# A feed-forward block begun with its first 256 rows, attention maxima turned on 64x32 tiles, and splits moved to VectorE, in a fused adaLN, attention and GLU kernel

## The chip, the cores and the metric

The kernel runs on one core of one Trainium2 chip. The time is that of the device, in microseconds from the start to the end of one execution. Before the change it is 1716.86 us, the median of three runs (1716.64 to 1719.71).

## The reference

One sequence of 2048 rows with 512 values each goes through attention and then through a gated feed-forward block, each behind a norm that is scaled and shifted by values computed from a condition vector `c`.

```python
mod = (silu(c) @ w_mod).reshape(1, 6, 1, 512)
sa, ca, ga, sb, cb, gb = ...
h = layernorm(x) * (1 + ca) + sa
q = heads(h @ wq)              # 32 heads of 16
k, v = h @ wk, h @ wv          # one head of 16, shared
p = softmax(q @ k.T * 16 ** -0.5)
x = x + ga * ((p @ v) @ wo)
h = layernorm(x) * (1 + cb) + sb
x = x + gb * ((sigmoid(h @ w_gate) * (h @ w_up)) @ w_down)   # 1792 wide
```

All is float32. The kernel splits most operands of its products into a high and a low float16 part and adds three products (high by high, high by low, low by high).

## The kernel before, in words

**A prologue** (`PLAN`) computes the norm, `k`, `v` and the first six of sixteen query groups, and writes the queries to DRAM (`qD`).

**The loop.** The queries are cut into 8 blocks of 256 rows (`NQ`), each with 4 groups of 8 heads (`NU`): 32 *units* (`units`, index `i`; block `b`, group `o`). A unit has 16 *steps*, one for each block of 128 keys (`NKB`), so there are 512 steps, `s`. A step has two halves (`h`), and `ORDER` fixes what each half issues:

- two tiles `sa` (scores with the queries on the partitions), 21 steps ahead of their use; VectorE reduces each 128x512 tile to its maxima (`mx`, in `a_max`);
- two tiles `st` (scores with the keys on the partitions, with the maximum subtracted through two extra rows of `qp`); ScalarE turns each into `P` with `Exp` (`st_tile`);
- one product `craw` of `P` with `V` in float32, two steps later (`pv`);
- one *piece* of other work (`piece`).

TensorE is used as eight tiles of 64 rows by 32 columns: `columns` (L133 is the line through which every operation of the prologue and loop is recorded) issues one product as four matmuls, one for each 32 columns of the output. `sa` and `st` of a half use one half of the rows, `craw` the other.

**Maxima.** Once a unit's last score tile is issued, `max_end` reduces `mx` (128 partitions, 8 heads x 2 blocks of 128 queries x 4 key chunks) to `m16` of 128x16, and `max_rows` turns it with one float32 matmul against the identity into 16x128, scales it on ScalarE, splits it into `mh`, and four DMAs on SP's queue write it into rows of `qp`.

**Other work: Groups, Couples, terms.** A `Group` is an accumulation of terms into one PSUM bank; a `Couple` runs two Groups together, each *term* on both halves of the rows, that is eight matmuls of 64x32 by 512 columns. The feed-forward work of a *pair* of query blocks (512 rows, `ffn_groups`) is: two Couples `wo` of 24 terms (the projection), the norm of the four row tiles (`norm`, `norm2`, `normed`, through `defer`, which runs a function some steps later), four pieces `tr` of transposes (`Transposes`, `tr_part`) whose result `split_evac` evicts as `h2` high and low, fourteen Couples `gu` of 24 terms (gate and up for one 128-wide chunk of 1792, one bank each), four of them behind two Couples `dn` of 48 terms, and at the end two of 36: 552 terms. In the norm, the sum `xr` and all after the statistics run on GpSimd (POOL), `bn_stats` on VectorE. Gate and up weights come from DRAM (`wD`) by `load_gw`, 512 KB a chunk, into `GWB` buffers.

**The planner.** `plan` picks a Couple when no piece is left, and `places` spreads its terms over the coming halves: `RATE` 2.2 terms a half, at most about 3; query Couples before step `FIRST` go at `QRATE` and skip three halves. `pick` takes the head of the list `main`: `wo` from nine steps (`SKIP`) after it was listed, `tr` two steps (`GAP`) after the norm's mark, others when the list `spare` is empty. Otherwise it takes from `spare`, where the five query Couples lie at first and where the last two `dn` Couples of each pair go (`KEPT`), to fill the time in which the next pair waits. A pair is listed when its second query block has been finished, at steps 128, 256 and 384. A Couple that wouldn't end within the loop isn't begun.

**Weights.** `weight_jobs` loads and splits `wo`, gate, up and down on POOL, 42 jobs over `WSTEPS` = 110 steps, and the last four (they overwrite the query weights) three steps apart from step `WLAST`.

**The tail** works without tiles (L184: 128x128 by 512 columns): the rest of `wo` of the fourth pair, `last_unit`, the first Couple left over, the end of `wo` (with norm), all others left over, the transposes, and the fourth pair's gate, up and down.

Of the kernel before, what the change touches and what calls it, by code (L numbers as in the profile page):

```python
# [16 lines left out]
P = 128  # L17
# [5 lines left out]
QB = 512  # L23
# [52 lines left out]
W1 = 2  # L76
W2 = 3
# [1 line left out]

PBUFS = 4  # L80
SBANKS = {"st": 2, "sa": 3}
GWB = 3
HBUFS = 36


# [1 line left out]
def adaln_mqa_glu_kernel(  # L87
# [39 lines left out]
    class Ordered:  # L127
        def __init__(self, engine):
            self.engine = engine
# [220 lines left out]
    def split_evac(src, k, sc, sh, hi, lo):  # L350
        h32 = t32("h32")[:, :QU]
        act.activation(h32, src, AF.Identity, scale=sc[:, k:k + 1], bias=sh[:, k:k + 1])
        pool.tensor_scalar(hi, h32, 1.0, 0.0, op0=ALU.mult, op1=ALU.add)  # L353
        pool.tensor_tensor(lo, h32, hi, op=ALU.subtract)  # L354


# [243 lines left out]
    pend = []  # L600

    def max_end(i):
        m16 = wp.tile([P, 16], F32, tag="m16", name="m16", bufs=4)
        dve.tensor_reduce(m16.rearrange("p (h t) -> p h t", t=2), mxs[i], axis=AX.X, op=ALU.max)
        return lambda: max_rows(i, m16)

    def max_rows(i, m16):
        qp = get_q(i)
        pm = sbank("sa")
        pe.matmul(pm[:16, :P], m16, ident, start=True, stop=True)  # L610
        m32 = wp.tile([16, P], F32, tag="m32", name="m32", bufs=4)
        act.activation(m32, pm[:16, :P], AF.Identity, scale=1.0 / SM)
        mh = wp.tile([16, 2, P], F16, tag="mh", name="mh", bufs=4)
# [127 lines left out]
    def defer(n, f_):  # L741
        waits.append((now[0] + n, f_))
# [34 lines left out]
    class Transposes:  # L777
        stage, n = "tr", 4

        def __init__(self, part):  # L780
            self.part = part

        def alone(self):
            self.part(0, 4)
# [1 line left out]
    def ffn_groups(b):  # L786
# [4 lines left out]
        gws = {}  # L791
        ths = {}
        fs = [*range(4, NFC), *range(4)]

        def wo_group(t):
            def term(n, rs):
# [24 lines left out]

        def norm(t, t1, xr):
            pool.tensor_tensor(xr, t1, xr, op=ALU.add)
# [12 lines left out]

        pts2 = {}

# [14 lines left out]
        def load_gw(f):  # L853
            if f < NFC:
                gws[fs[f]] = gw_tile()
                sp1.dma_start(gws[fs[f]], wD[fs[f]])

        def gu_group(p, m):
            def term(n, rs):
                k, i = divmod(n, 3)  # L860
                gw = gws[fs[p]]
                w_, h_ = passes(gw[:, 2 * m], gw[:, 2 * m + 1], *h2[k])[i]
                return w_[rs, k, :], h_[rs]

            def end(p_, second):
                if m == 0:
                    ths[p] = th = t32("th")
                    act.activation(th, p_, AF.Tanh, scale=0.5 / (SH * SW))  # L868
                else:
                    th = ths.pop(p)  # L870
                    if second:
                        u_ = t32("u")
                        dve.tensor_copy(u_, p_)
                        pool.tensor_scalar(th, th, 1.0, 1.0, op0=ALU.add, op1=ALU.mult)  # L874
                        pool.tensor_tensor(th, th, u_, op=ALU.mult)
                    else:
                        dve.scalar_tensor_tensor(th, th, 1.0, p_, op0=ALU.add, op1=ALU.mult)
                    hi, lo = t16("gh"), t16("gl")
                    pool.tensor_scalar(hi, th, 1.0, 0.0, op0=ALU.mult, op1=ALU.add)
                    pool.tensor_tensor(lo, th, hi, op=ALU.subtract)  # L880
                    gT[fs[p]] = (hi, lo)

            return Group("gu", 12, "pgu", term, end, (lambda: load_gw(p + GWB - 1)) if m == 0 else None)

        HF = 8

        def down_group(t, lo):
            n_ = HF if lo == 0 else NFC - HF
# [23 lines left out]
            return Group("dn", 3 * n_, "pd", term, end)  # L912

        wos = [wo_group(t) for t in range(4)]
        trs = [Transposes(lambda n0, n1, u=u, z=z: tr_part(u, z, n0, n1)) for u in range(2) for z in range(2)]
        gs = []
        for lo, hi in ((0, HF), (HF, NFC)):
            gs += [Couple(gu_group(p, 0), gu_group(p, 1)) for p in range(lo, hi)]
            gs += [Couple(down_group(t, lo), down_group(t + 1, lo)) for t in (0, 2)]
        return wos, trs, gs  # L920


    alist = [(i, n) for i in range(len(units)) for n in range(64)]
# [81 lines left out]
    first_rows = []  # L1005

    def pick(s):
        if first_rows and s >= (len(units) - NU) * NKB + SKIP:
            return first_rows.pop()
        while main and main[0][0] is None:  # L1010
            main.pop(0)
            spare.extend(z[1] for z in main[:KEPT])
            del main[:KEPT]
        if main:
            b, g = main[0]
            if g.stage == "tr":
                ok = b in marks and s >= marks[b] + GAP
            elif g.stage == "wo":
                ok = s >= g.ready + SKIP
            else:  # L1020
                ok = not spare
            if ok:
                return main.pop(0)[1]
        return spare.pop(0) if spare else None


    def plan(s, hb):
# [6 lines left out]
        if g.stage == "tr":  # L1034
            sizes = [4]
        else:
            q = g.stage == "q" and s < FIRST
            rate, most = (QRATE, 1) if q else (RATE, MOST)
            sizes = []
            for leg in range(2):  # L1040
                sizes += places(g.n // 2, hb + len(sizes), rate, most, (3 if leg == 0 else 0) if q else None, g.w)
            if hb + len(sizes) > 2 * len(units) * NKB:
                spare.insert(0, g)
                return
# [17 lines left out]
    for i, (b, o) in enumerate(units):  # L1062
        if o == 0 and b == NQ - 1:
            ends = ffn_groups(NB - 1)
            first_rows.append(Couple(*ends[0][:2]))
        if o == 0 and b > 0 and b % 2 == 0:
            pair = b // 2 - 1
            wos, trs, gs = ffn_groups(pair)
            gs = [Couple(*wos[:2]), Couple(*wos[2:])] + trs + gs
            for g in gs[:2]:  # L1070
                g.ready = i * NKB
            main.extend([(pair, g) for g in gs[:-KEPT]] + [(None, None)] + [(pair, g) for g in gs[-KEPT:]])
        for kb in range(NKB):
            s = i * NKB + kb
            now[0] = s
# [51 lines left out]
    del psum["s"]  # L1127
    pinned.clear()
    tail.append(True)
    wos, trs, gs = ends  # L1130
    assert not first_rows
    wos = wos[2:]
    for g in wos:
# [41 lines left out]
```

## Time and profile before

| what | us |
|---|---|
| median of three runs | 1716.86 |
| the profiled execution | 1717.44 |
| its span, first to last instruction | 1715.4 |
| start of the first `P` (step 0) | 109.0 |
| end of the last `P` (step 511) | 1553.3 |

The profiled execution is 2.0 us longer than its span, and 0.6 us longer than the median. The loop's 2048 tiles `P` mark its steps: four to a step. A view of windows counts them, and the time of a window over a quarter of its tiles is the time of one step. Matmuls overlap, so a busy TensorE says little: what a term costs is seen in the length of the steps and in the chain of work that ended last.

### The profile page before, as it was taken

Reading aid. Unit: us, or ns where it says so; the run is one execution under the profiler, and the core shown is the slowest. Engines: PE = TensorE matmul, PEld = TensorE weight load, DVE = VectorE, ACT = ScalarE, POOL = GpSimd, SP = SyncE. Lnnn points to the kernel's source line nnn. Section 1 sums busy time; section 2 is a strip of 40 time slices with the busy share of each in tenths; the row PEclk is TensorE's granted clock in tenths of the full one; section 3 lists DMA queues with packets and bytes.
Section 4 is the critical chain, followed back from the end, with each engine's and each line's share of the span. In section 5 each row is a group of like instructions: output and inputs, shape, how many; then the busy total and the mean of one; then the engine's idle time right before and its main releaser. Section 6 shows DMA issues by size and latency. Waiting matters only on the chain.

```text
span 1715.4 us, 88057 instructions
## 1 busy us (share of the span) xinstructions
PE 1667.8 (97%) x39888; PEld 996.6 (58%) x39888; DVE 1409.5 (82%) x2364; ACT 1290.5 (75%) x2335; POOL 616.3 (36%) x812
## 2 busy tenths in 40 slices
PE   6999999999999999999999999999999999999998
PEld 3335554555564667666765666666666666654443
DVE  7799999999998999999998999999998999802111
ACT  5448988999987888888887888888888888882100
POOL 4432545452047332132254222233364233221523
PEclk9989999999999999999999999999999999999999
DMA  7111323321022111010121110010112110011211
GB/s 247 47 61 48 102 94 111 92 70 33 15 64 63 49 45 32 12 50 27 28 65 52 52 40 28 25 44 20 38 50 63 47 57 15 24 50 47 82 54 49
DMA packets 84675, 94.06 MB, mean 55 GB/s; under 512 B 22868, under 2 KB 63820, under 8 KB 84300
## 3 DMA queue, kind: packets, MB, share of 16 engines
q1 hardware_dynamic: 84300, 88.44, 16.6%
q8 instruction: 312, 5.11, 1.2%
q14 instruction: 63, 0.52, 0.1%
HBM read 67.82 MB, written 16.24 MB: 49 GB/s over the span
## 4 chain that ended last, share of the span: by engine, by line
PE 85%; DVE 5%; ACT 3%; POOL 3%; DMA 1%; issue 1%; SPq 1%; POOLq 0%; ACTq 0%; DVEq 0%
PE craw L133 23%; PE pgu L133 15%; PE sa L133 14%; PE st L133 13%; PE pd L133 6%; PE pgu L184 5%; DVE mx L133 3%; PE pd L184 3%; PE po L133 2%; PE pq L133 2%; ACT P L133 2%; SPq L133 1%; DMA lc<-lD 1%; POOL h2l L354 1%; DMA xall<-in_A_x_dram 1%
## 5 line engine op out<-in xcount | busy, mean ns | idle before, releaser
L133 DVE TENSOR_REDUCE mx<-sa 128x1 f32<-128x512 f32 x2048 | 1293.4, 683 | 99.2 <-PE st L133 43.5
L133 ACT ACTIVATE P<-st 128x512 f32<-128x512 f32 x2048 | 1166.7, 598 | 221.3 <-PE st L133 163.9
L133 PE MATMUL craw<-P,V 64*32 64x512 f32 x8192 | 1096.2, 601 | 1.2 <-PE craw L133 0.2
L133 PE MATMUL sa<-kp,qp 64*32 64x512 f16 (+1 forms) x7940 | 837.0, 379 | 10.9 <-DVE mx L133 10.3
L133 PE MATMUL st<-qp,kp 64*32 64x512 f16 x8192 | 838.6, 380 | 7.9 <-ACT P L133 6.2
L133 PEld LDWEIGHTS <-kp 64*32 64x32 f16 x8192 | 336.4, 91 | 227.9 <-issue 105.7
L133 PEld LDWEIGHTS <-qp 64*32 64x32 f16 (+1 forms) x7940 | 286.0, 92 | 132.6 <-issue 55.1
L133 PE MATMUL pgu<-h2h,gw 64*32 64x512 f16 x4992 | 268.8, 377 | 3.4 <-POOL h2h L353 2.6
L133 PEld LDWEIGHTS <-gw 64*32 64x32 f16 x7488 | 171.6, 92 | 69.1 <-issue 29.4
L133 PEld LDWEIGHTS craw<-P,V 64*32 64x32 f32 x8192 | 184.7, 105 | 26.9 <-ACT cs L133 4.6
L133 PE MATMUL craw<-nought 64*32 64x1 f16 x1048 | 171.2, 163 | 0.0
L133 PE MATMUL pgu<-h2l,gw 64*32 64x512 f16 x2496 | 167.4, 377 | 1.0 <-POOL h2l L354 1.0
L133 PEld LDWEIGHTS <-nought 64*32 64x32 f16 x1048 | 97.8, 93 | 72.0 <-issue 53.4
L874 POOL TENSOR_SCALAR th<-th 128x512 f32<-128x512 f32 x39 | 24.2, 620 | 315.3 <-ACT th L133 263.3
L554 POOL MEMSET qp<- 32x1024 f16 x60 | 56.6, 944 | 117.8 <-PE st L133 83.7
L184 PE MATMUL pgu<-h2h,gw 128*128 128x512 f16 x272 | 81.4, 379 | 2.2 <-POOL h2h L353 2.2
L318 POOL TENSOR_SCALAR wst<-wst 128x512 f32<-128x512 f32 x46 | 28.4, 618 | 153.5 <-DMA wst<-in_B_w_up_dram 106.4
L868 ACT ACTIVATE th<-pgu 128x512 f32<-128x512 f32 x17 | 10.1, 597 | 94.3 <-PE pgu L184 94.1
L133 PE MATMUL pd<-wdl,gh 64*32 64x512 f16 x1152 | 75.7, 376 | 0.0
L133 PE MATMUL pd<-wdh,gh 64*32 64x512 f16 x1152 | 75.0, 376 | 0.2
L133 PE MATMUL pd<-wdh,gl 64*32 64x512 f16 x1152 | 73.7, 376 | 0.0
L704 POOL TENSOR_TENSOR raw<-raw 128x256 f32<-128x256 f32 x31 | 22.7, 732 | 139.1 <-DMA raw<-lD 131.6
(159 smaller groups left out, 1438.7 us busy)
## 6 DMA issues: line engine op xcount, KB each, us to landing
gw<-wD SPq DMA_DIRECT2D x56, 512.0 KB
wD<-gw SPq DMA_DIRECT2D x14, 512.0 KB
wm<-in_w_mod_dram SPq DMA_DIRECT2D x6, 1024.0 KB
qp<-qD SPq DMA_DIRECT2D x192, 32.0 KB
qD<-q SPq DMA_DIRECT2D x16, 256.0 KB
xr<-in_A_x_dram SPq DMA_DIRECT2D x16, 256.0 KB
out_dram<-ot SPq DMA_DIRECT2D x16, 256.0 KB
raw<-cs SPq DMA_DIRECT2D x248, 16.0 KB
```

Of the source, the lines that this page charges most:

```text
L133: return (lambda *a, **k: keep(f_(*a, **k))) if pinned else f_
L184: pe.matmul(cut[0](self.bank) if cut else self.bank, l_, r_, start=(n == 0), stop=(n == self.n - 1))
L318: pool.tensor_scalar(w_, w_, SW, 0.0, op0=ALU.mult, op1=ALU.add)
L354: pool.tensor_tensor(lo, h32, hi, op=ALU.subtract)
L554: eng.memset(qp[j:j + 32], 0.0)
L704: keep(pool.tensor_tensor(raw[:, :QU], raw[:, :QU], raw[:, QU:], op=ALU.mult))
L868: act.activation(th, p_, AF.Tanh, scale=0.5 / (SH * SW))
L874: pool.tensor_scalar(th, th, 1.0, 1.0, op0=ALU.add, op1=ALU.mult)
```

## The change

- Each of the first three pairs is listed in two parts. When the first of its query blocks is finished (steps 64, 192, 320), its first `wo` Couple, the two transposes of these 256 rows and Couples `gu_half` are listed: gate and up of two chunks at once, each product 256 columns wide, 48 terms at a weight of one half. `AHEAD` = 4, 3, 3, 0 Couples of this kind, that is 8, 6, 6 and 0 chunks. When the second block is finished (128, 256, 384), the other `wo`, its transposes, the same chunks for the other 256 rows (the weights are loaded again), the rest of gate and up, and `dn` follow.
- Before step 137 such a Couple goes at `ERATE` = 1.2 (at most 2) instead of 2.2.
- Query Couples go at 0.9 a half instead of 0.45, and count as early before step 77 instead of 136; the last four weight jobs begin at step 115 instead of 150.
- `norm2` comes two steps after `norm` instead of one. A mark is set for each 256 rows, and the transposes alternate between them.
- `split_evac` makes the high part with a copy on VectorE instead of on POOL.
- `max_end` makes two reductions of 64 partitions, and the turn is a matmul of 64 rows by 32 columns over 64 columns; `mh` is 32x64, and each DMA takes 16 rows of it.
- `GWB` is 4 instead of 3, and weights are asked for one Couple further ahead.

```diff
-QRATE = 0.45
+QRATE = 0.9
+ERATE = 1.2
+AHEAD = 4, 3, 3, 0
-WLAST = 150
+WLAST = 115
-FIRST = 136
+FIRST = 77
-GWB = 3
+GWB = 4
...
     def split_evac(src, k, sc, sh, hi, lo):
         h32 = t32("h32")[:, :QU]
         act.activation(h32, src, AF.Identity, scale=sc[:, k:k + 1], bias=sh[:, k:k + 1])
-        pool.tensor_scalar(hi, h32, 1.0, 0.0, op0=ALU.mult, op1=ALU.add)
+        dve.tensor_copy(hi, h32)
         pool.tensor_tensor(lo, h32, hi, op=ALU.subtract)
...
-        m16 = wp.tile([P, 16], F32, tag="m16", name="m16", bufs=4)
-        dve.tensor_reduce(m16.rearrange("p (h t) -> p h t", t=2), mxs[i], axis=AX.X, op=ALU.max)
+        m16 = wp.tile([64, 32], F32, tag="m16", name="m16", bufs=4)
+        for u in range(2):
+            dve.tensor_reduce(m16.rearrange("p (h t u) -> p h t u", t=2, u=2)[:, :, :, u], mxs[i][64 * u:64 * u + 64],
+                              axis=AX.X, op=ALU.max)
...
-        pe.matmul(pm[:16, :P], m16, ident, start=True, stop=True)
+        pe.matmul(pm[:32, :64], m16, ident[:64, :64], start=True, stop=True)
...
-                    sp1.dma_start(qp[r:r + 1], mh[8 * j:8 * j + 8, h, :])
+                    sp1.dma_start(qp[r:r + 1], mh[16 * j:16 * j + 16, h, :])
...
+        ahead = 2 * AHEAD[b]
+        uses = [(p, 0) for p in range(ahead)]
+        uses += [(p, None) for p in range(NFC)]
...
-            defer(1, lambda: norm2(t, t1, xr))
+            defer(2, lambda: norm2(t, t1, xr))
...
-            if t == 3:
-                marks[b] = now[0]
-                for f in range(GWB - 1):
-                    load_gw(f)
+            if t % 2 == 1:
+                marks[b, t // 2] = now[0]
+            if t == (1 if ahead else 3):
+                ask(2 if ahead else GWB - 1)
...
+        def gu_half(p, m, u, at):
+            us = slice(u * QU, (u + 1) * QU)
+
+            def term(n, rs):
+                e, (k, i) = n // 12, divmod(n % 12, 3)
+                gw = gws[at + e]
+                w_, h_ = passes(gw[:, 2 * m], gw[:, 2 * m + 1], *h2[k])[i]
+                return w_[rs, k, :], h_[rs, us], lambda z: z[:, e * QU:(e + 1) * QU]
+
+            def end(p_, second):
+                gated(p, m, p_, second, [(e, us, slice(e * QU, (e + 1) * QU)) for e in range(2)])
+
+            return Group("gu", 24, "pgu", term, end, (lambda: ask(at + GWB)) if m == 0 else None, w=0.5)
...
+        es = [Couple(gu_half(p, 0, 0, p), gu_half(p, 1, 0, p)) for p in range(0, ahead, 2)]
+        gs += [Couple(gu_half(p, 0, 1, at + p), gu_half(p, 1, 1, at + p)) for p in range(0, ahead, 2)]
...
-            rate, most = (QRATE, 1) if q else (RATE, MOST)
+            light = not q and g.stage == "gu" and s < 2 * NU * NKB + SKIP
+            rate, most = (QRATE, 1) if q else (ERATE, 2) if light else (RATE, MOST)
...
-        if o == 0 and b > 0 and b % 2 == 0:
-            pair = b // 2 - 1
-            wos, trs, gs = ffn_groups(pair)
-            gs = [Couple(*wos[:2]), Couple(*wos[2:])] + trs + gs
...
+        if o == 0 and b % 2 == 1 and b < NQ - 1:
+            blocks[b // 2] = ffn_groups(b // 2)
+            wos, trs, _, es = blocks[b // 2]
+            main.extend([*ready(b // 2, [Couple(*wos[:2]), trs[0], trs[2]], i), (None, len(es)), *ready(b // 2, es, i)])
+        if o == 0 and b % 2 == 0 and b > 0:
+            wos, trs, gs, _ = blocks.pop(b // 2 - 1)
+            gs = [Couple(*wos[2:]), trs[1], trs[3], *gs]
+            main.extend([*ready(b // 2 - 1, gs[:-KEPT], i), (None, KEPT), *ready(b // 2 - 1, gs[-KEPT:], i)])
```

More of the change, by code (lines that the diff above doesn't have):

```diff
@@ L778, in adaln_mqa_glu_kernel, with __init__ @@
         stage, n = "tr", 4
-        def __init__(self, part):
-            self.part = part
+        def __init__(self, part, u):
+            self.part, self.u = part, u
         def alone(self):
@@ L865, in end @@
             def end(p_, second):
[L866 to L885, printed above, removed]
+                gated(p, m, p_, second, [(0, slice(0, QB), slice(0, QB))])
+            return Group("gu", 12, "pgu", term, end, (lambda: ask(at + GWB)) if m == 0 else None)
         def down_group(t, lo):
@@ L1003, in places, with ready @@
         return [k - z for z, k in zip([0] + ends, ends)]
-    first_rows = []
+    first_rows, blocks = [], {}
+    def ready(pair, gs, i):
+        for g in gs:
+            g.ready = i * NKB
+        return [(pair, g) for g in gs]
     def pick(s):
@@ L1010, in pick @@
         while main and main[0][0] is None:
-            main.pop(0)
-            spare.extend(z[1] for z in main[:KEPT])
-            del main[:KEPT]
+            n = main.pop(0)[1]
+            spare.extend(z[1] for z in main[:n])
+            del main[:n]
         if main:
@@ L1129, in adaln_mqa_glu_kernel @@
     tail.append(True)
-    wos, trs, gs = ends
+    wos, trs, gs, _ = ends
     assert not first_rows
```

57 lines of the change are left out of this document (40 added, 17 removed).

## The prediction

> **What bounds the kernel now.** I read the windows first, cut at the units of the loop by the times of the tiles `P`: for `P` alone, then for all engines (columns: window, its us, busy us and count of PE, PEld, DVE, ACT and, in the second, POOL, granted clock, DMA share, GB/s). In the first view VectorE has no column, since it touches no `P`.
>
> ```profile
> 109.00:478.80 369.80, 304.46 (x2280) 45.02 (x2280) 320.58 (x576) 0.99 0.22 67
> 624.60:809.50 184.90, 136.71 (x1028) 24.52 (x1024) 147.56 (x257) 1.00 0.12 35
> ```
> ```profile
> 109.00:478.80 369.80, 364.23 (x8143) 191.25 (x8140) 357.68 (x603) 330.69 (x610) 138.37 (x176) 0.99 0.22 67
> 624.60:809.50 184.90, 184.48 (x5474) 125.70 (x5467) 171.86 (x279) 154.61 (x279) 51.85 (x59) 1.00 0.12 35
> 1553.30:1715.40 162.10, 152.71 (x727) 69.55 (x722) 29.52 (x50) 14.91 (x27) 54.29 (x64) 1.00 0.18 59
> ```
>
> 576 tiles are 144 steps: 369.8 / 144 = 2.57 us a step while only queries run beside the attention, and VectorE is busy for 97% of it. 256 tiles (the 257th is the next window's) are 64 steps: 2.89 us a step while gate, up and down run; VectorE is at 93%, ScalarE at 84%. There the matmuls number 5474; 16 each of `sa`, `st` and `craw` a step make 3 x 1028, and some 130 are hand-overs, so (5474 - 3084 - 130) / 8 = 282 terms ran, 4.4 a step. The early window has 120 query terms over some 140 steps, 0.83 a step, with matmuls counted the same way. So **a term costs (2.89 - 2.57) / (4.4 - 0.83) = 0.09 us in the loop**: early VectorE sets the pace and TensorE has room, later they share it.
>
> The tail is another matter. The chain of work that ended last shows it:
>
> ```profile
> 1563.83 6.91 PE pgu L184 x32
> 1570.73 1.30 PE po L184 x6
> 1572.03 8.63 PE pgu L184 x40
> 1580.66 15.55 PE pd L184 x72
> 1597.01 1.26 POOL ot L905
> 1599.39 1.11 POOL h2h L353 x3
> 1602.56 40.31 PE pgu L184 x186
> ```
>
> 72 matmuls take 15.55 us, **0.216 us a term**. The 32 + 40 `pgu` and 72 `pd` ahead of 1602.56 are 144 terms of the third pair that the loop had no room for. A term moved from the tail into the loop is worth 0.216 - 0.09.
>
> Third, three places in the loop are slower than their neighbours, each at the norm and the transposes of a pair (again `P` alone):
>
> ```profile
> 517.20:546.50 29.30, 19.39 (x136) 2.76 (x128) 17.98 (x32) 0.88 0.21 66
> 908.60:922.60 14.00, 7.32 (x52) 1.32 (x48) 6.75 (x12) 0.88 0.34 102
> 1280.30:1292.90 12.60, 6.58 (x56) 1.05 (x48) 7.18 (x13) 1.00 0.22 56
> ```
>
> 8, 3 and 3 steps at 2.89 us would be 23.1, 8.7 and 8.7: **15.4 us of stalls**. In the chain of the second one the work passes to POOL:
>
> ```profile
> 908.85 1.28 POOL ot L899
> 910.13 2.46 POOL ot L905 x2
> 912.59 0.38 POOL h2h L353
> 913.05 0.67 POOL h2l L354
> ```
>
> POOL finishes the eviction of `dn` first, then makes eight high and eight low parts, and gate and up wait.
>
> **The change part by part**, against the profiled execution's 1717.4 us (0.6 above the median).
>
> *Terms in the first 137 steps.* Five query Couples at 0.9 instead of 0.45 end by step 76. Then come one `wo` Couple (24 terms), two transposes, and four half Couples of 48 x 0.5 at 1.2 a half, ten steps each, so all four end near step 131. That is 240 terms there instead of 112, and 128 x 0.09 = 11.6 us. From below: TensorE has room, and the step pays only what VectorE gets.
>
> ```profile
> L133 DVE TENSOR_TENSOR t<-po,ga 128x512 f32<-128x512 f32 x7 | 4.8, 681 | 0.0
> L133 DVE BATCH_NORM_STATS2 st<-xr 128x6 f32<-128x512 f32 x14 | 9.6, 684 | 3.7 <-POOL xr L823 3.5
> L133 DVE BATCH_NORM_AGGREGATE mv<-st 128x2 f32<-128x6 f32 x30 | 5.5, 182 | 1.0
> L133 DVE COPY u<-pgu 128x512 f32<-128x512 f32 x39 | 26.6, 682 | 38.6 <-PE pgu L133 38.6
> ```
>
> One 0.68, two 0.68 + 0.18 and four 0.68 are 5.1 us, and four copies for the splits 1.4 more (below): 6.5. **I take +9.** The faster queries give VectorE nothing; ScalarE and POOL evict them.
>
> *Terms after step 137.* By the planner's rules 1524 instead of 1544 run there: 20 x 0.09, **-1.8**. In the list above, work of the next pair is now listed when a pair ends some 27 steps sooner, so the loop stays filled; two waits of eight steps for a norm remain empty (near 142 and 272).
>
> *The tail.* Of 1680 terms (3 x 552 and the fourth pair's first `wo`) the planner's rules leave one `dn` Couple, 36 terms, at the loop's end. So 108 x 0.216 = 23.3 us go. But the 24.2 us of work from 1572.03 to 1596.21 covered the norm of the last two row tiles, whose VectorE part the timeline bounds:
>
> ```profile
> 1571.49 0.69 DVE L811 TENSOR_TENSOR t<-po,ga 128x512 f32<-128x512 f32 x1 [1.70 <-PE po L184]
> 1578.87 0.55 DVE L348 TENSOR_SCALAR t<-xr,mv,rs 128x512 f32<-128x512 f32 x1
> ```
>
> 1579.4 - 1572.0 = 7.4 us are bare once no work is left there; what is late next is the transposes. Half of these (256 rows ready long before) fit in the wait, and of the 6.35 us from 1596.21 to 1602.56 some 2.3 go with that half and with POOL's high parts. The first Couple left over grows from 24 to 36 terms: 2.6. So -24.2 + 7.4 - 2.3 + 2.6 = **-16** (from -23.3, nothing bare, to -9, if the wait is twice as long).
>
> *Stalls.* The eight high parts leave POOL (0.40 us of 1.07 each), the rows come in halves, the last weight jobs leave the first stall, and the order lets `dn` run behind the transposes of the first halves of pairs two and three. Against it, there are six places instead of three. I take 1 us at each: **-10** (from -15.4 to +15.4, should all six stay as long).
>
> *The split on VectorE* isn't in the trace with this shape. The nearest rows:
>
> ```profile
> L133 DVE CAST wkvh<-wkv 128x128 f16<-128x128 f32 x1 | 0.2, 226 | 0.0
> L353 POOL TENSOR_SCALAR h2h<-h 128x256 f16<-128x256 f32 x32 | 12.6, 404 | 0.7 <-ACT h L133 0.7
> ```
>
> It lies between 0.23 (half as wide, the same operation) and 0.68 (twice as wide, out of PSUM, above); I take 0.35, by the first. Twenty in the windows where VectorE is at 93% find room. The copy is an added wait: VectorE stands until ScalarE has made `h`, behind one `Exp` at most, and the next maxima queue up behind it, for which `sa` waits once three banks are full. The -10 above holds this.
>
> *Maxima.* Per unit:
>
> ```profile
> L133 DVE TENSOR_REDUCE m<-mx 128x16 f32<-128x64 f32 x32 | 7.0, 219 | 1.0
> L133 DVE TENSOR_TENSOR mh<-m,mh 16x128 f16<-16x128 f32 x32 | 11.0, 345 | 3.4 <-ACT mh L133 3.4
> L133 PE MATMUL sa<-ident,m 128*16 128x128 f32 x64 | 12.5, 278 | 0.0
> ```
>
> A second reduction adds up to 0.22 on VectorE, 64 columns for 128 in `mh` take up to 0.17 off, and the matmul no longer needs both halves of the rows (up to 0.56 of 2 x 0.278). Over 32 units that is from -23 to +7. Near VectorE's rows, **+2** for these and the late copies. The Trainium skill, TensorEngine Tiling, Key Properties, says that a change of tiling mode drains TensorE; by it the turn would save more than its own time, towards the lower end. No row here isolates a drain.
>
> *Products of 256 columns.* 960 terms of half width stand where 480 ran, 768 of them after step 137, each with its own eight weight loads. Two take as long as one of 512 if the loads (0.092 us) hide under 0.108 of stream:
>
> ```profile
> L133 PEld LDWEIGHTS <-gw 64*32 64x32 f16 x7488 | 171.6, 92 | 69.1 <-issue 29.4
> 1548.48 0.40 PE L133 MATMUL st<-qp,kp 64*32 64x512 f16 x4
> 61.67 1.30 PE pv L133 x48
> ```
>
> Four tiles whose matmuls take 0.38 each are through in 0.40, so tiles start some 7 ns apart; a full array with short products starts one every 1.30 / 48 = 27 ns. If the latter held for tiles too, a half term would take 8 x 27 ns = 0.216, no less than a whole one. From 0 to 768 x 0.108 = +83 us; the second row has the kernel's own tiles, so I stay near it: **+4** (5 ns each).
>
> The 20 chunks loaded twice are 10 MB more where DMA is at 0.12 to 0.22; each is asked for one Couple ahead. A load that waits for its buffer holds up on SP's queue the rows of `mh`, `place` and the loads of `raw` behind it; these have two steps or more. I cost them at nothing, and at up to a step a Couple, 20 x 2.9, if the cover goes.
>
> **Sum:** +9 - 1.8 - 16 - 10 + 2 + 4 = -12.8; 1717.4 - 12.8 = 1704.6, and 0.6 less for the median: **1704**.
>
> **The rivals.**
>
> *Slower: tiles have an issue floor.* In the 90 steps with half terms after 137, 8.5 of them a step with 50 other matmuls make 118; at 27 ns that is 3.2 us against 2.89, and +0.31 x 90 = 28. It decides from 24.4 ns a matmul (2.89 / 118) on. 1704 - 4 + 28 = **1728**; with all of the +83, 1783. For it: that row, and that the kernel never needed more: 184.9 us / 5474 is 34 ns a matmul. Against it: the row of four tiles in 0.40. Chance 0.2. The Trainium skill, TensorE: Matmul & The Clock Gate, "Wait — 56ns, not 53.3ns?", gives a floor of about 25 ns from start to start however narrow the product; the trace agrees on the full array. By that figure a half term is 0.2, 118 matmuls 2.95 us, and the time 1704 - 4 + 0.06 x 90, an estimate of 1705. The same page's span model has some 4 ns for each further tile, and by that nothing is added.
>
> *Slower: six stalls for three.* A wait takes the place of the one removed: if the transposes' evictions hold each of six places for 5.1 us, +15.4 replaces -10: **1729**. For it: the chain ends at `h2l`, which stays on POOL. Against: half the rows at a time. Chance 0.1.
>
> *No gain: the leftovers were cover.* If the norm's wait is twice as long (tail -9), the early terms cost 11.6 and the stalls give 8 back: 1704 + 7 + 2.6 + 2 = **1715.6**. For it: the bare norm is one chain over VectorE and POOL, with nothing beside it; against it, its 7.4 us were measured with other work on VectorE. Chance 0.13.
>
> *More.* Early terms at 6.5, the tail at -20, stalls at -15, turns at -3: **1687**. For it: the early window is VectorE's (97%), so its own sum may be all that counts there. Chance 0.17.
>
> **How the numbers follow.** The forecast (1696 to 1712) has 0.4, the rivals 0.2, 0.1, 0.13 and 0.17. The range 1686 to 1736 leaves out the far end of the floor and a little below, under 0.2. A measurement tells about 0.2% from no change, so the same is 1713.4 to 1720.3: the third rival holds most of it. Faster 0.4 + 0.17 + 0.03 = 0.6; same 0.12; slower 0.28.
>
> **What would show it.** Steps before 137 up to 2.7 us; no `pgu` of the third pair in the tail, 36 `pd`, and some 7 us of idle TensorE ahead of the transposes; no window of three steps with 5 us beyond 2.89. If steps with half terms go beyond 3.1 us, the floor is real and the forecast wrong; likewise if the stalls come back six times.

## The result, and the profile after

The changed kernel takes **1777.65 us** (median of four runs, 1775.27 to 1781.07) against 1716.75 for the kernel before (four runs, 1714.72 to 1719.71): a ratio of 1.0355, with a 95% interval from 1.0332 to 1.0378. It is 3.6% slower, where 1704 was forecast, and it lies beyond the upper end of the range, 1736. The profiled execution took 1777.78 us with a span of 1776.0.

From the page after, the busy times, the instruction queue, the shares of the chain and the group of half-width products:

```profile
PE 1680.3 (95%) x44488; PEld 1044.8 (59%) x44488; DVE 1436.1 (81%) x2427; ACT 1297.0 (73%) x2336; POOL 619.2 (35%) x827
...
q8 instruction: 348, 5.70, 1.4%
...
PE 81%; DVE 8%; ACT 4%; issue 3%; SPq 1%; POOL 1%; DMA 1%; POOLq 0%; ACTq 0%; DVEq 0%
...
L135 PE MATMUL pgu<-h2h,gw 64*32 64x256 f16 (+1 forms) x7936 | 327.4, 309 | 20.1 <-issue 19.0
```

The first three of these on the page before:

```profile
PE 1667.8 (97%) x39888; PEld 996.6 (58%) x39888; DVE 1409.5 (82%) x2364; ACT 1290.5 (75%) x2335; POOL 616.3 (36%) x812
...
q8 instruction: 312, 5.11, 1.2%
...
PE 85%; DVE 5%; ACT 3%; POOL 3%; DMA 1%; issue 1%; SPq 1%; POOLq 0%; ACTq 0%; DVEq 0%
```

TensorE has 44488 matmuls, and as many weight loads, where it had 39888, yet is busy for only 12.5 us more. The last two lines after tell more. "issue" is 3% of the chain of work that ended last, where the kernel before had 1%. The group of the last line had 20.1 us of idle time before it, 19.0 of it ended by "issue" (it holds 2816 products of 512 columns too, but by shape all of the 19.0 lies before the 5120 narrow ones): TensorE stood, and nothing that the profile shows held it. That is this case.

Where the time went, by windows cut at the starts of the tiles `P` (us; steps with half-width work after step 137 in bold). The last column is an experiment, told below, that has half as many products, of 512 columns, in place of the half-width ones.

| steps | before | after | as 512 columns |
|---|---|---|---|
| 0 to 72 | 189.0 | 190.5 | 190.6 |
| 73 to 88 | 41.2 | 46.0 | 45.1 |
| 89 | 2.5 | 14.0 | 12.8 |
| 90 to 131 | 107.2 | 115.7 | 112.9 |
| **151 to 172** | 69.8 | 81.4 | 64.9 |
| **251 to 266** | 46.1 | 57.7 | 46.5 |
| **281 to 296** | 51.7 | 59.1 | 46.9 |
| **385 to 426** | 125.2 | 142.0 | 121.8 |
| steps 0 to 510 in all | 1441.8 | 1520.7 | 1452.2 |
| tail, from the start of step 511 | 164.6 | 146.6 | 146.7 |

The tail gives back 18.0 us, where 16 were forecast. The loop takes 78.9 more.

First the bold rows. Two windows of the kernel after, all engines, in the columns of the prediction (window, its us, PE, PEld, DVE, ACT, POOL, clock, DMA share, GB/s): steps 90 to 131, where `ERATE` puts some five half terms into a step, and 151 to 172, where `RATE` puts in eight or nine.

```profile
359.20:474.90 115.70, 112.97 (x3653) 75.20 (x3636) 109.48 (x184) 100.49 (x182) 53.53 (x73) 1.00 0.22 66
526.20:607.70 81.50, 69.09 (x2635) 51.41 (x2624) 62.29 (x103) 54.48 (x98) 18.65 (x28) 0.98 0.20 64
```

Steps 151 to 172 of the kernel before, with the first pair's stall in them:

```profile
499.50:569.30 69.80, 65.68 (x1589) 35.87 (x1583) 60.68 (x106) 55.41 (x104) 48.81 (x74) 0.95 0.20 63
```

In the first of the kernel after, 3653 matmuls in 42 steps are 87 a step, 2.75 us each. In the second, 2635 in 22 steps are 120 a step, and a step takes 3.70 us with **no engine busy for more than 85%**: TensorE 69.09 of 81.50, VectorE 62.29, ScalarE 54.48. The chain in 526.3 to 607.7 has its shares, and a short stretch of it (from 587.5) shows how they come about (start, us, what):

```profile
by line: PE pgu L135 36.7%; PE craw L135 20.0%; issue 15.4%; PE sa L135 15.1%; PE st L135 11.1%; ACT P L135 1.5%; ACT th L135 0.3%
```
```profile
587.98 0.70 PE pgu L135 x33
...
589.45 0.64 PE pgu L135 x38
...
590.90 0.15 PE pgu L135 x2
591.05 2.04 issue
593.10 0.61 PE pgu L135 x27
```

38 narrow matmuls are through in 0.64 us, 17 ns each, so they start fast enough. Then TensorE stops for 2.04 us, in the middle of one product's terms, and goes on as fast as before. What runs out, as the following shows, is the instructions. The view of DMA for 588.5 to 591.0 (queue: packets, MB, share of the engines):

```profile
q1 hardware_dynamic: 320, 0.91, 92.1%
q8 instruction: 1, 0.02, 2.4%
```

The one packet of the instruction queue in it has 16384 bytes. By the trace's records it was sent at 590.75, 5.6 us after the one before (585.12), while the loads of two chunks of `gw`, and at the end one of `raw`, took 92% of the DMA engines. It landed at 591.70, and TensorE resumed 1.4 us later. The next ones were sent at 594.17 and 597.64, 3.4 and 3.5 us apart. Over the whole trace there are 348 such packets for 2 x 44488 instructions of TensorE, 255.7 each; in the kernel before, 312 for 2 x 39888, again 255.7. So **TensorE's instructions come in blocks of 256**, and a step of 120 matmuls and as many weight loads uses up 240 in what should be 2.85 us. In the records of every kernel of this case the shortest distances between two blocks are 3.2 to 3.5 us.

The records of single instructions show that the pauses belong to these blocks. In 88 places of the loop after, TensorE starts neither a matmul nor a weight load for over 0.5 us; 50 of these pauses (49.2 us) end 1.2 to 1.6 us after a block has landed, which would be so for some 8% by chance. In the kernel before, 2 of 28 do (1.1 us). From the end of one of the 50 to the end of the next, TensorE runs 254 to 256 matmuls and weight loads in 31 of the 49 cases; all 40 counts under 1300 lie within two of a multiple of 256. In the bold rows these pauses add up to 44.5 us.

Second, step 89, a single step of 14.0 us. Its window for `P` alone, and the timeline of POOL (start, us, instruction, idle time before it and what ended that):

```profile
345.20:359.20 14.00, 3.50 (x24) 0.40 (x16) 2.42 (x5) 0.64 0.50 174
```
```profile
328.52 2.52 POOL L832 TENSOR_TENSOR xr<-t,xr 128x512 f32<-128x512 f32 x2
336.74 0.62 POOL L320 TENSOR_SCALAR wst<-wst 128x512 f32<-128x512 f32 x1 [5.70 <-DMA wst<-in_B_w_up_dram]
...
343.17 0.62 POOL L320 TENSOR_SCALAR wst<-wst 128x512 f32<-128x512 f32 x1 [3.86 <-DMA wst<-in_B_w_down_dram]
...
345.81 0.25 POOL L338 TENSOR_SCALAR ve<-mv 128x1 f32<-128x1 f32 x1
...
347.92 2.09 POOL L350 TENSOR_SCALAR t<-xr,mv,rs 128x512 f32<-128x512 f32 x1
...
352.20 2.09 POOL L350 TENSOR_SCALAR t<-xr,mv,rs 128x512 f32<-128x512 f32 x1
```

POOL has the sums `xr` of the first pair's early rows at 331.0. Two weight splits stand ahead of the norm's last steps in its queue, and they wait 5.70 and 3.86 us for their loads; so the norm is ready at 354.3, and the transposes of TensorE, and behind them the scores, stand for it.

Third, the tail, the chain from 1642.49 on:

```profile
1642.49 7.77 PE pd L186 x36
1650.26 0.66 PE po L186 x3
...
1650.97 0.64 DVE t L820
...
1652.27 1.29 DVE xr L822 x2
...
1653.77 1.20 DVE st L335 x2
...
1657.20 0.47 DVE t L350
...
1657.71 2.20 PE pt L854 x9
...
1660.88 39.24 PE pgu L186 x176
```

36 `pd` and no `pgu` are left of the third pair, and the norm is bare from 1650.92 to 1657.71, 6.8 us.

### The profile page after: what moved, and what is told of

The parts are those of the page before. It is cut to its first block, busy times and chain, and to the rows that moved or that the text cites. A ratio compares the mean times of both kernels' runs of the same rounds, so it can differ in the third digit from the quotient of the medians.

```text
span 1776.0 us, 97425 instructions
## 1 busy us (share of the span) xinstructions
PE 1680.3 (95%) x44488; PEld 1044.8 (59%) x44488; DVE 1436.1 (81%) x2427; ACT 1297.0 (73%) x2336; POOL 619.2 (35%) x827
## 4 chain that ended last, share of the span: by engine, by line
PE 81%; DVE 8%; ACT 4%; issue 3%; SPq 1%; POOL 1%; DMA 1%; POOLq 0%; ACTq 0%; DVEq 0%
PE craw L135 22%; PE pgu L135 15%; PE sa L135 14%; PE st L135 11%; PE pd L135 7%; DVE mx L135 6%; PE pgu L186 4%; PE pd L186 2%; PE po L135 2%; PE pq L135 2%; ACT P L135 2%; SPq L135 1%; DMA xall<-in_A_x_dram 1%; DVE st L135 1%; PE pt L135 0%
## 5 line engine op out<-in xcount | busy, mean ns | idle before, releaser
L135 PE MATMUL st<-qp,kp 64*32 64x512 f16 x8192 | 850.1, 380 | 12.0 <-ACT P L135 7.0
L135 PE MATMUL sa<-kp,qp 64*32 64x512 f16 (+1 forms) x7940 | 846.5, 380 | 14.2 <-DVE mx L135 9.0
L135 PE MATMUL pgu<-h2h,gw 64*32 64x256 f16 (+1 forms) x7936 | 327.4, 309 | 20.1 <-issue 19.0
L135 PEld LDWEIGHTS <-gw 64*32 64x32 f16 x11904 | 251.2, 91 | 107.6 <-issue 58.7
L135 PE MATMUL pgu<-h2l,gw 64*32 64x256 f16 (+1 forms) x3968 | 226.3, 309 | 11.0 <-issue 10.9
L135 PE MATMUL pd<-wdh,gh 64*32 64x512 f16 x1248 | 84.9, 378 | 0.2
L135 PE MATMUL pd<-wdl,gh 64*32 64x512 f16 x1248 | 84.8, 377 | 0.0
L320 POOL TENSOR_SCALAR wst<-wst 128x512 f32<-128x512 f32 x46 | 28.6, 621 | 150.2 <-DMA wst<-in_B_w_up_dram 77.2
L135 PEld LDWEIGHTS <-gh 64*32 64x32 f16 x2496 | 64.6, 92 | 18.2 <-issue 5.4
L904 POOL TENSOR_TENSOR gl<-th,gh 128x256 f16<-128x256 f32 (+1 forms) x76 | 68.3, 905 | 4.7
```

The lines of the kernel that those rows point to most:

```text
L135: return (lambda *a, **k: keep(f_(*a, **k))) if pinned else f_
L320: pool.tensor_scalar(w_, w_, SW, 0.0, op0=ALU.mult, op1=ALU.add)
L904: pool.tensor_tensor(lo[:, to], th[:, of], hi[:, to], op=ALU.subtract)
```

## The experiments

The theory is that the half-width products use up instructions faster than blocks arrive (the supply theory), with the loads of twice fetched chunks delaying some blocks further. The expectations call it theory A. Its main rival, their theory B, is akin to the prediction's own: a narrow product has a price of its own on the array, wherever it stands. Times of single runs below can be some 5 us off: the kernel before, run beside them, lay between 1711.85 and 1723.47. Steps and windows of one profile are finer.

**`h_wide`: the same stream, half the instructions.** After, with each half Couple as 24 terms of 512 columns instead of 48 of 256. The same 256 columns of `h2` are read twice, and half of the products are left out. Couples, loads and evictions stay.

```diff
-                e, (k, i) = n // 12, divmod(n % 12, 3)
-                gw = gws[at + e]
+                k, i = divmod(n, 3)
+                gw = gws[at + (k >= 2)]
-                return w_[rs, k, :], h_[rs, us], lambda z: z[:, e * QU:(e + 1) * QU]
+                return w_[rs, k, :], h_[rs, us].unsqueeze(1).to_broadcast([64, 2, QU])
-            return Group("gu", 24, "pgu", term, end, (lambda: ask(at + GWB)) if m == 0 else None, w=0.5)
+            return Group("gu", 12, "pgu", term, end, (lambda: ask(at + GWB)) if m == 0 else None)
```

> The changed kernel with the half Couples as 24 terms of 512 columns (the same 256 columns of h2 read twice; half of the terms of each of its chunks are left out, so gate and up of these chunks are not what the reference has). Stream time, weight traffic from DRAM, evictions and plan stay; weight loads and matmuls of these Couples are halved. In the changed kernel the four stretches of half terms after step 137 (steps 151-173, 251-267, 281-297, 385-427) take 66.6 us more than 2.85 us a step. Theory A (TensorE's instructions arrive in blocks of 256, about 3.5 us each, and half terms need 240 instructions a step): these stretches fall to 2.9 us a step, time about 1712. Theory B (a product of 256 columns is too short to hide its weight load on the array): the same, about 1712. Theory C (gate and up weights loaded twice, two chunks at once, or evictions hold these stretches): no change, 1777.

1712.35 us. The window of steps 151 to 172, all engines:

```profile
524.30:589.20 64.90, 64.37 (x1883) 43.32 (x1872) 60.02 (x103) 53.31 (x98) 18.64 (x28) 1.00 0.25 79
```

86 matmuls a step, 2.95 us, and TensorE busy throughout. The four bold rows of the table are 16.5, 11.2, 12.2 and 20.2 us shorter than after: 60.1 in all, of 65.5 between the two spans. So the loss comes with the narrow products, and not with the order of the work, the loads, the evictions or the lists, which stay. Whether their number of instructions or their width costs the time, this run can't tell, since it changes both; A and B forecast the same here.

**`h_64`: fewer, wider tiles.** After, with the half Couples' products as two matmuls of 64x64 instead of four of 64x32; nothing is left out.

```diff
-    def columns(dst, l_, r_, start, stop):
-        for c_ in range(0, P, 32):
+    def columns(dst, l_, r_, start, stop, w_=32):
+        for c_ in range(0, P, w_):
-                    columns(cut[0](g.bank) if cut else g.bank, l_, r_, n == 0, n == 2 * m - 1)
+                    columns(cut[0](g.bank) if cut else g.bank, l_, r_, n == 0, n == 2 * m - 1, 64 if cut else 32)
```

> The changed kernel with the half Couples on tiles of 64x64 instead of 64x32: half the weight loads and matmuls, products still 256 columns wide, all else the same. Theory A (supply of instructions): the stretches fall to about 2.9 us a step plus what changes between 64x32 and 64x64 tiles cost (0 to 0.4 us a step): 1712 to 1745. Theory B (short products don't hide the weight loads, which are longer here): no faster, 1777 or more. Theory C (traffic, evictions): 1777.

1748.9 us. The same steps:

```profile
526.80:599.30 72.50, 72.44 (x1878) 37.49 (x1876) 63.83 (x103) 55.15 (x98) 18.58 (x28) 1.00 0.21 70
```

As many instructions as in `h_wide`, and the pauses are gone (TensorE is busy for 72.44 of 72.50, and "issue" has 0.4% of the chain), though the products are as narrow as in the kernel after. But a step takes 3.30 us, 0.35 more than in `h_wide`, and the time is 4 us above the supply theory's range (1712 to 1745), about what a single run can be off. These 0.35 us don't show as idle time. They may be the changes between tiles of 64x32 and 64x64 in each half, or the narrow products' own weight loads; neither was tried by itself.

**`b_split`: the suspect alone.** Before, with gate and up of the second pair as two products of 256 columns each: no other part of the change.

```diff
-                    columns(g.bank, l_, r_, n == 0, n == 2 * m - 1)
+                    for z in range(0, QB, QU if g.two else QB):
+                        zs = slice(z, z + (QU if g.two else QB))
+                        columns(g.bank[:, zs], l_, r_[:, zs], n == 0 and z == 0, n == 2 * m - 1 and (z > 0 or not g.two))
+            g.two = b == 1
```

> The kernel before, with gate and up of the second pair alone (14 Couples, about 77 steps) issued as two products of 256 columns for each of 512, each with its own weight load; no other part of the change. Theory A and B: these steps go from 2.88 to about 3.65 us, +60 us: about 1775. Theory C: no change, 1717. In the trace A wants bursts with a matmul every 13.5 ns and pauses in which TensorE waits for nothing shown, each ending a fixed time after a block of instructions has landed; B wants evenly longer spacing and no pauses.

1772.62 us, by this one edit. The steps 297 to 384 (253.5 us before), and the first line of TensorE's waits (us in total, times, longest), which has no like among those of the kernel before:

```profile
937.70:1235.70 298.00, 275.00 (x9829) 194.33 (x9813) 242.41 (x384) 216.02 (x384) 73.60 (x84) 1.00 0.11 32
```
```profile
PE pgu L133 <- issue: 17.1, 28, 1.7
```

112 matmuls a step, 3.39 us, at a DMA share of 0.11. Here no chunk is loaded twice, so the supply falls short by itself. This is also where A and B part: B wanted evenly longer spacing without pauses, A pauses behind blocks. Of the 33 pauses of over 0.5 us in these steps, 32 (28.6 us) end 1.2 to 1.6 us after a block landed, where the steps are 44.5 us longer than before.

**`a_traffic`: fewer bytes.** After, loading one quarter of each chunk of the half Couples, both times, which stands in the products for all four. That is less than the kernel before loads for these chunks.

```diff
-                sp1.dma_start(gws[k], wD[fs[uses[k][0]]])
+                if k < 2 * ahead:
+                    sp1.dma_start(gws[k][:, 0], wD[fs[uses[k][0]]][:, 0])
+                else:
+                    sp1.dma_start(gws[k], wD[fs[uses[k][0]]])
-                w_, h_ = passes(gw[:, 2 * m], gw[:, 2 * m + 1], *h2[k])[i]
+                w_, h_ = passes(gw[:, 0], gw[:, 0], *h2[k])[i]
```

> The changed kernel with only a quarter of each chunk's weights loaded for its half Couples (128 KB instead of 512; this quarter stands for the other three in their products, so gate and up of these chunks are not the reference's). Instructions stay. In the changed kernel blocks of TensorE's instructions land every 4.07 us in the first stretch of half terms, not every 3.4, and its longest pauses (2.0 us) fall together with the loads of weights. Theory A with contention: the blocks wait behind these loads, so the stretches fall from 3.65 towards 3.4 us a step (240 instructions, 3.4 to 3.5 us a block), 10 to 25 us: 1752 to 1767. Theory A without contention: the same 3.65, 1777. Theory C (traffic is all): 1712.

1762.83 us, within the expectation. Steps 151 to 172:

```profile
522.00:598.50 76.50, 67.39 (x2643) 50.27 (x2639) 62.62 (x103) 54.22 (x98) 18.61 (x28) 1.00 0.13 37
```

The same 120 matmuls a step take 3.48 us instead of 3.70. In these steps the blocks are sent 3.70 us apart on the mean, after 3.92. But these 5.0 us are most of what the bold rows gain: the other three fall by 0.6, 1.0 and 1.5, so 8.1 of 60 in all, and the pauses behind blocks there are as long as before (45.2 us for 44.5). The whole is 14.8 us faster (one run), the rest of it spread over the loop. So the loads explain the smaller part of the loss at most.

**`a_slow`: the same instructions, spread.** After, with half Couples past step 137 at 1.5 (at most 2) a half instead of 2.2 (at most 3).

```diff
-            rate, most = (QRATE, 1) if q else (ERATE, 2) if light else (RATE, MOST)
+            rate, most = (QRATE, 1) if q else (ERATE, 2) if light else (1.5, 2) if g.w < 1 else (RATE, MOST)
```

> The changed kernel with its half Couples after step 137 at 1.5 (at most 2) instead of 2.2 a half: 6 half terms a step instead of 8.5, so 98 matmuls and as many weight loads instead of 118. Theory A (TensorE's instructions come in blocks of 256, one in 3.4 us at the earliest): 196 instructions a step need a block only every 3.7 us, so the pauses go and these steps fall from about 3.65 to 2.9 us, although nothing else about them changes. Theory B (on the array a half term costs as much as a whole one): 6 whole terms a step took 3.1 to 3.2 us before, so 3.1 or more. The planner leaves 144 terms for the tail (36 in the changed kernel), so the time is about 1728 by A and 1755 by B.

1754.11 us: the total is where the rival had it. Steps 151 to 172 are 66.8 us, of which the last ones no longer hold half terms:

```profile
529.90:596.70 66.80, 62.42 (x2165) 43.78 (x2155) 58.93 (x101) 53.66 (x96) 14.69 (x22) 1.00 0.19 61
```

The 131 steps with half terms take 3.04 us on the mean and 2.87 at the median, most with six half terms and some 100 matmuls. Their commonest length is 2.61 us, and some with the same six terms take over 4. TensorE's waits for "issue" at `pgu` fall from 29.8 to 9.3 us. A fixed price per matmul, the kernel after's 3.70 / 120 = 31 ns, would make 3.1 us of 100, and that is near the mean, though not 2.61 and 4 for the same work. My expectation from the supply theory (2.9 us a step) was missed by 26 us in the total: each of the 131 steps is 0.19 above 2.85 (24 us), and 144 terms are left for a tail of 163.2 us. This run alone doesn't decide; the spread of the steps speaks for supply, their mean and the total don't.

**`a_none`: the change without its half Couples.**

```diff
-AHEAD = 4, 3, 3, 0
+AHEAD = 0, 0, 0, 0
```

> The changed kernel with no half Couples at all (0 chunks ahead for every pair); first wo and first transposes still go ahead, and queries, maxima, splits and norm are as changed. By the planner's rules 96 terms are left for the tail instead of 36 (144 before). All theories: the 66.6 us and the 8 us of steps 90-131 go, 13 us come back in the tail, less 5 to 7 of cover: about 1710. The stop of 11.5 us at step 89 stays, since the first transposes are there still: if it goes too, it came from the half Couples.

1711.4 us (five runs), 0.9944 of the kernel before (0.9920 to 0.9968). Steps 151 to 172:

```profile
516.90:580.40 63.50, 63.34 (x1883) 43.37 (x1872) 59.73 (x103) 53.21 (x98) 17.87 (x22) 1.00 0.16 47
```

2.89 us a step, and the stall of 69.8 - 63.5 = 6.3 us that the kernel before had there is gone. Step 89 still takes 13.3 us: the stop has nothing to do with narrow products.

**`a_none_l4` and `a_late`: the stop.** Two edits of `a_none`. The first makes the splits wait longer behind their loads; the second lists the first pair's early `wo` 32 steps later, behind most of the weight jobs, and starts the last four of these nine steps later.

```diff
-WLATE = 2
+WLATE = 4
```

> The kernel without half Couples, with each weight split four steps after its load is issued instead of two. In the changed kernel the stop of 11.5 us at step 89 has POOL waiting for the load of a w_down block that SP's queue issued late, with the norm's steps queued behind that split. Theory: with two steps more POOL doesn't wait, the stop shrinks to 2 or 3 us, and the time falls by 8 to 1703. Rival (the stop is POOL's own work, splits and norm): it stays within 2 us, 1710.

1708.22 us (six runs), 0.9948 (0.9931 to 0.9965), the same as `a_none`. Step 89 takes 12.3 us, and POOL still waits, 5.43 and 2.41 us: SP issues the load of the `w_up` block only at 332.04, behind eight loads of `raw`, and POOL goes on at 335.34; the splits' distance doesn't mend that. This idea failed. The rival of its expectation, that POOL's own work makes the stop, isn't refuted by it.

```diff
-WLAST = 115
+WLAST = 124
-            main.extend([*ready(b // 2, [Couple(*wos[:2]), trs[0], trs[2]], i), (None, len(es)), *ready(b // 2, es, i)])
+            main.extend([*ready(b // 2, [Couple(*wos[:2]), trs[0], trs[2]], i + (2 if b == 1 else 0)), (None, len(es)), *ready(b // 2, es, i)])
```

> The kernel without half Couples, with the first pair's early wo listed 32 steps later (so its norm falls behind the 42 weight jobs, at about steps 111 to 117) and the last four weight jobs at step 124. If the stop at step 89 is POOL's queue, where the norm stands behind weight splits that wait for loads issued late on SP's queue, it goes: 1711 - 10 to 13, 1698 to 1701. If it comes with the transposes wherever they stand, it moves to step 119: 1711.

**1699.1 us** (four runs, 1696.85 to 1699.71), 0.9888 of the kernel before (0.9867 to 0.9908): faster than both kernels. Step 89:

```profile
336.90:339.30 2.40, 2.40 (x58) 1.24 (x50) 2.40 (x5) 2.16 (x5) 2.23 (x3) 1.00 0.72 251
```

Steps 73 to 88 fall from 46.4 to 41.2 us, step 89 from 13.3 to 2.5, and steps 90 to 131 rise from 106.7 to 110.3. So the stop goes when the first rows don't come among the weight jobs. In the kernel after, 14.8 us lie between the sums `xr` and the norm's next step on POOL: 9.6 of waits for loads (5.70 and 3.86), the rest the splits themselves. In `a_late` it is 2.1, and the longest step at that norm takes 4.03 us (step 118).

**Single parts, each in the kernel before.** `b_max` has the maxima's diff alone, `b_norm` the high parts on VectorE and the later `norm2`, `b_q` the queries and weight jobs:

```diff
-QRATE = 0.45
+QRATE = 0.9
-WLAST = 150
+WLAST = 115
-FIRST = 136
+FIRST = 77
```

> The kernel before with the maxima turned on 64x32 tiles alone. By the prediction's sum about 0 to +1 us (a second reduction of 0.22 us a unit on VectorE against a matmul that needs only half of the rows). A rival by which changes of tiling stop TensorE would have some 3 to 9 us off: 1708 to 1714.

1713.74 us (12 runs), 0.9982 (0.9969 to 0.9995): some 3 us faster, the near end of the rival's range. The groups of its trace that answer to the three rows of the prediction:

```profile
L133 DVE TENSOR_REDUCE m<-mx 64x16 f32<-64x64 f32 x64 | 13.6, 213 | 1.4
L133 DVE TENSOR_TENSOR mh<-m,mh 32x64 f16<-32x64 f32 x32 | 11.0, 345 | 3.6 <-ACT mh L133 2.7
L133 PE MATMUL sa<-ident,m 64*32 64x64 f32 x64 | 9.4, 226 | 0.0
```

VectorE pays 13.6 - 7.0 = 6.6 us and saves nothing at `mh` (345 ns at either shape). The step with the turn (the twelfth of a unit) is longer in the early window, 3.08 for 2.91 us, and shorter later, 3.06 for 3.25 (steps 160 to 479), where TensorE sets the pace. That it is the change of tiling, and not the shorter matmul, isn't shown.

> The kernel before with the high parts of the splits on VectorE and norm2 one step later, nothing else. The three stalls (15.4 us over 2.89 us a step) held POOL's eight high parts: these shrink by 0.4 x 8 = 3 us each if POOL is what ends last, so 1717 - 8 = 1709; if the eviction of dn on POOL ahead of them is the larger part, only some 4 us go: 1713. If VectorE pays for the copies it gives up to 8 back.

1718.17 us (12 runs), 1.0002 (0.9988 to 1.0017): nothing. The windows at the first two pairs' stalls shrink a little (69.8 to 66.3, 51.7 to 50.5), the third not, and the total keeps none of it: in its profile the loop is 3.1 us shorter and the tail 2.7 longer. The expectation of 4 to 8 us less failed, and why isn't settled.

> The kernel before with the faster queries alone (0.9 a half, early until step 77) and the last weight jobs at step 115. The same terms run; the first 137 steps should cost the same (0 to +2 us), and the first stall (steps 157 to 164, 6 us) should lose what the weight jobs at steps 150 to 159 add, some 3 to 5 us: 1712 to 1716.

1706.75 us (six runs), 0.9932 (0.9916 to 0.9949), better than expected: the loop takes 1435.7 for 1441.8 us, the window at the first stall 65.6 for 69.8, and 120 terms instead of 144 are left for a tail of 159.5 (164.6 before).

## Why the prediction was wrong

**The step that failed is "Products of 256 columns", +4.** The cost is 60 us (`h_wide` against after, the four bold rows) to 65 (their spans). I argued that a half term is free if weight loads hide under the stream and tiles start some 7 ns apart. The term's own bounds went from 0 to +83 us, and I took its low end by a row that shows only how fast tiles start. The burst of 38 in 0.64 us agrees that starts don't limit. What I didn't count is that each matmul and each load is an instruction that has to be brought in. At 3.3 to 3.5 us for 256, the bound was in the trace before: its page has 312 instruction packets of 5.11 MB, and I neither divided 2 x 39888 by 312 nor compared the distances of the packets. With whole terms a step uses 2 x 86 = 172 instructions, 2.2 to 2.4 us of supply under a step of 2.85; 240 need 3.1 to 3.3. The rest up to 3.70 is blocks that come late; the loads make 0.22 of it (`a_traffic`), and what delays them otherwise isn't known.

The Trainium skill, Runtime: NRT & Kernel Launch, "Instruction fetch mechanics", has instructions fetched in 16 KiB blocks of 256, which both traces confirm at 255.7 a packet. It holds that fetching is hidden, since instructions are issued more slowly than they arrive. With these tiles the measurement says otherwise: "issue" is 15.4% of the chain in steps 151 to 172.

**The rival "tiles have an issue floor" had the rate nearly right, the cost at less than half, and the mechanism wrong.** Its 27 ns a matmul is 256 instructions, 128 matmuls, in 3.46 us: the same rate, but a mean over bursts of 17 ns and pauses. Its 3.2 us for 118 matmuls is near the supply's own bound, and it had 1728 because it left out the late blocks and took 90 steps at 0.31 (28 us, where 60 were lost). The sign that I had named for it, steps of over 3.1 us, came (3.70), but it doesn't show a floor: pauses that lie multiples of 256 instructions apart give the same sign.

**"20 chunks loaded twice", at nothing, was somewhat low:** some 8 of these 60 us go when the loads shrink to a quarter, and 15 in the whole run (`a_traffic`). No product waits for its buffer in the list of TensorE's waits, as I had argued; that the loads hold up blocks is seen at one place (5.6 us at a DMA share of 92%) and likely elsewhere.

**"Stalls", -10, was right in number at the pairs, by means that aren't shown, and missed the stop at step 89.** In `a_none` the windows 151 to 172 and 281 to 296 are 6.3 and 4.6 us shorter than before (63.5 and 47.1), and the third pair's (127.4 for 125.2) isn't: -8.7 for the three. The term was built on the high parts that leave POOL and on the halves. Yet `b_q`, with neither, shortens the same windows by 9.1 us (to 65.6, 47.3 and 124.7), and `b_norm`, with the high parts, by 4.2; so the agreement may be luck. And I moved the norm of the first early rows into the steps in which POOL splits weights, and didn't count that it stands behind them there: +11.5 at step 89 and +4.8 in the 16 steps ahead. `a_late` takes both away.

**Early terms, +9:** 1.5 in steps 0 to 72 and 8.5 in 90 to 131 make +10.0. Right in number; of the 8.5, 2.7 go in `h_wide` and so belong to the narrow products.

**The tail, -16:** -18.0. Its three steps came as told: 36 `pd` and no `pgu` are left, the norm is bare for 6.8 us (7.4 forecast), and `pgu` starts 10.0 us after the last `po` (30.5 before).

**Maxima and late copies, +2:** the sign was wrong, -3 by `b_max`, with no cost of the copies to be seen in `b_norm`. The copy of the high part takes 0.29 us (0.35 forecast), by the tile's own row in the trace after:

```profile
L135 DVE CAST h2h<-h x24: 277/294/1367, 355.9 to 1332.6; 128x256 f16<-128x256 f32 x24
```

Put together: without the failed term the forecast was 1700. With the stop's 10.3 + 3.9 = 14.2 us in `h_wide` that makes 1714; `h_wide` took 1712.35. And without half Couples and stop, `a_late` takes 1699.1. So the terms beside these two add up, though single ones are off by up to 5 us and partly cancel; the two (60 and 14 us) make the 74 us between 1704 and 1777.65. The -1.8 for terms after step 137 is too small to be seen by itself.

What stays open: that a new block is asked for only once one has been used up is inferred from the distances of at least 3.2 us and from the next block's start, 1.1 to 1.2 us after most of the 50 pauses; no run tests it by itself. Open too is the rest of the 60 us beyond the 44.5 in pauses of over 0.5 us. So are `b_norm`'s nothing and the 26 us of `a_slow`.

## What to carry to other kernels

Before cutting products narrower, count instructions: matmuls and weight loads per step against the blocks in which they come (the instruction queue's packets on the page), and not stream cycles alone. Gaps of TensorE that end with "issue" while no engine is full, behind a packet of the instruction queue and a multiple of its instructions apart, are the sign. When a norm or any chain over a shared queue is moved earlier, look at what else that queue does at the new place, above all what waits there for loads.

## What the runs showed of the hardware that was not expected

- TensorE's supply: blocks of 256 instructions, at best 3.2 to 3.5 us apart in any kernel here, some 25 to 27 ns for a matmul with its weight load. On the mean of steps 151 to 172 it was 3.92 us, 3.70 with a quarter of the loads of `gw`, and 5.6 at one place beside two of them.
- Where the supply falls short, TensorE's pauses lie 256 instructions or a multiple of that apart, and they end 1.2 to 1.6 us after a block has landed.
- 38 matmuls of 64x32 by 256 columns are through in 0.64 us, as long as instructions are there.
- Products of 256 columns as 64x64 tiles among tiles of 64x32 made steps 0.35 us longer than products of 512 columns on 64x32 tiles with the same number of matmuls (3.30 against 2.95 us).
